# A decode block that streams 561 MB: fewer and larger first and last loads, one VectorE product per group, and the first load issued before the engines' blocks

## The chip, the cores and the metric

The kernel runs on one core of a Trainium2 chip. The metric is the device time of one execution in microseconds (us). The kernel before took 1305.1 us (median of 3 runs, 1304.54 to 1305.36).

## The reference

One decode step for 4 sequences: attention over a cache of 4096 positions with 32 heads of 128, plus a small mixer and MLP, all on the layer-normalised input.

```python
xn = _layernorm(x)                                   # x: 4 x 1 x 512
q  = (xn @ wq).reshape(4, 1, 32, 128)                # per head
s  = einsum("bhqd,bhkd->bhqk", q, k_cache) * 128 ** -0.5
o  = einsum("bhqk,bhkd->bhqd", softmax(s), v_cache)  # k_cache, v_cache: 4 x 32 x 4096 x 128, f32
A  = o.reshape(4, 1, 4096) @ wo
B  = x1 + gelu(_layernorm(x1) @ w3) @ w4             # x1 = xn + the mixer's part
out = x + A + B
```

With one position per sequence, the shifts of the mixer push everything out, so its two weights have no influence, x1 is xn, and the kernel doesn't load them.

## The kernel before

Keys and values are 268 MB each. They are cut into 32 groups of 8.39 MB: a group is four heads of one sequence, laid out as 128 partitions with 16,384 f32 each. Three buffers of that size take turns: S1 and S0 hold keys (even and odd groups), S2 holds values. The weights pass through the same buffers: wq goes through S2 before the first values, w3 and w4 go to S1 after the last even keys, wo goes to S0 after the last odd keys. x and its small intermediates sit at the start of S0 until the second keys are loaded over them.

All large loads are issued by SyncE, on one queue, in the order in which they are written (lines 125 to 157): wq in two pieces of 12/32 and 20/32 (GF = 12), the first keys in two halves, the second keys after `d_T` (q is ready), then a loop over pairs of groups: values when S2 is free (`v_free`), keys when a key buffer is free (`k_free`). At the end come w3, four rows of w4, the last values in two pieces of 12/32 and 20/32, the remaining ten rows of w4, and wo in six pieces. Since SyncE issues in order, a load that waits holds up all loads behind it. x is loaded by ScalarE on its own queue (line 226).

The work on a group:

- VectorE (lines 333 to 353) spreads q over the partitions (qx, qb), multiplies the keys by it in place (two halves, lines 343 and 345), sums over the 128 dimensions (line 347; then `k_free`) and finds the maximum of the scores (lines 349 to 352).
- ScalarE (lines 240 to 248) takes the exponential of the scores into pw.
- TensorE (lines 195 to 209) multiplies the values by pw: 32 matmuls of 512 columns, which the trace counts as 64 passes, then the sums of the weights (then `v_free`), then, after a copy by ScalarE (os), the small products that pick the heads (oz).

The wq product runs on the same TensorE code as turn 0 of 33, with pw holding the transposed input; so both wq and the last values, which come in two pieces, need a wait in the middle of the 32 matmuls (`take(v_rest)` at n = GF, line 199). GpSimd relays these second pieces: it waits for them and then adds to `v_rest`, once with the number of groups, so that the wait passes in all turns between (lines 171 to 176). The same is done for the second half of the first keys (`s_kh`, `s_h`). Matmul GF - 1 of each turn adds to `v_half`; SyncE waits for it before it overwrites the first piece of S2 with that of the last values.

The MLP's first product (w3) runs before the last turn of TensorE; its second (w4, line 217) after it, then X, the normalised attention output, is transposed, and the output product (from line 370) takes wo piece by piece, adds everything, and two small stores write the result.

Of the kernel before, what the change touches and what calls it, by code (L numbers as in the profile page):

```python
# [13 lines left out]
P = 128  # L14
# [6 lines left out]
def decode_block(ctx: ExitStack, tc: tile.TileContext, x, k, v, wq, wo, w3, w4, out):  # L21
# [45 lines left out]
    def sem(name):  # L67
        return tc.alloc_semaphore(name)

    def take(e, s, n=1):  # L70
        e.wait_ge(s, n).then_inc(s, -n)  # L71
# [1 line left out]
    PIECES = ((0, 14), (14, 22), (22, 27), (27, 30), (30, 31), (31, 32))  # L73
    CUT = 27
    SUM = 30
    GF = 12
    s_x, s_v, s_q, s_w3, s_w4 = (sem(n) for n in ("sx", "sv", "sq", "sw3", "sw4"))
    s_k = [sem(f"sk{n}") for n in range(2)]
    s_wo = s_k + [s_x] + [sem(f"swo{n}") for n in range(3)]
    d_self, g_a, c_done, d_T, k_free, v_free, v_rest, v_half = (sem(n) for n in ("dself", "ga", "cd", "dT", "kf", "vf", "vr", "vh"))  # L80
    s_kh, s_h = sem("skh"), sem("sh")
    d_a, a_d, p_a, a_p, d_p, p_d = (sem(n) for n in ("da", "ad", "pa", "ap", "dp", "pd"))

    kf = k.rearrange("b h s d -> (b h s d)").rearrange("(g p r) -> g p r", g=NG, p=P)
# [23 lines left out]
        return e.matmul(o, l, r, start=start, stop=stop)  # L108

    nc.vector.addr_align(128, offset=4, max_nops=0)  # L110
    with tc.tile_critical(no_gpsimd_drain=True), nc.Block(no_gpsimd_drain=True) as block:

        @block.sync
        def _(e):
            def src(flat, g):
                return flat[g] if isinstance(g, int) else flat[bass.ds(g, 1)].rearrange("g p r -> (g p) r")

            def load_k(g, n):
                e.dma_start(KS[n][:, :], src(kf, g)).then_inc(s_k[n], 16)

            def load_v(g):
                take(e, v_free)
                e.dma_start(S2[:, :], src(vf, g)).then_inc(s_v, 16)

            FIRST, REST = slice(0, GF * 4 * DH), slice(GF * 4 * DH, ROW)
            wq_r = wq.rearrange("(p c) n -> p (c n)", p=P)
            e.dma_start(S2[:, FIRST], wq_r[:, FIRST]).then_inc(s_v, 16)
            e.dma_start(S2[:, REST], wq_r[:, REST]).then_inc(s_q, 16)
            for half, s in ((slice(0, ROW // 2), s_k[0]), (slice(ROW // 2, ROW), s_kh)):
                e.dma_start(S1[:, half], kf[0][:, half]).then_inc(s, 16)  # L130
            e.wait_ge(d_T, 1)
            load_k(1, 1)
            with nc.Fori(0, NG, 2, engines=[ET.SP]) as g:
                load_v(g)
                take(e, k_free)
                e.br_lt(g, NG - 2, on_true="sp_more", on_false="sp_next")
                with nc.body("sp_more", valid_engines=[ET.SP]):
                    after = nc.s_assert_within(g + 2, None, NG - 2,
                                               skip_runtime_bounds_check_because="the last turn skips this block")
                    load_k(after, 0)  # L140
                    load_v(after - 1)
                    take(e, k_free)
                    load_k(after + 1, 1)
                    nc.br("sp_next", engines=[ET.SP])
                nc.switch_bb("sp_next")
            e.dma_start(w3_sb, w3.rearrange("(p c) f -> p c f", p=P)).then_inc(s_w3, 16)
            w4_r = w4.rearrange("(p m) n -> p m n", p=P)
            e.dma_start(w4_sb[:, 0:4, :], w4_r[:, 0:4, :]).then_inc(s_w4, 16)
            e.wait_ge(v_half, NG)
            e.dma_start(S2[:, FIRST], vf[NG - 1][:, FIRST]).then_inc(s_v, 16)  # L150
            take(e, v_free)
            e.dma_start(S2[:, REST], vf[NG - 1][:, REST]).then_inc(s_q, 16)
            e.dma_start(w4_sb[:, 4:NF, :], w4_r[:, 4:NF, :]).then_inc(s_w4, 16)
            take(e, k_free)
            wo_r = wo.rearrange("(p c) n -> p c n", p=P)
            for n, (c0, c1) in enumerate(PIECES):
                e.dma_start(wo_sb[:, c0:c1, :], wo_r[:, c0:c1, :]).then_inc(s_wo[n], 16)  # L157

        @block.gpsimd
        def _(e):  # L160
            e.memset(xs, 0.0).then_inc(g_a, 1)
            e.memset(ident[:, :], 0.0).then_inc(c_done, 1)
            e.memset(rs[:, :], 0.0)
            e.memset(pw[:, :, :], 0.0)
            e.wait_ge(c_done, 1)
            e.affine_select(out=ident[:, :], in_=ident[:, :], compare_op=ALU.not_equal, fill=1.0, base=0,
                            pattern=[[-1, P]], channel_multiplier=1).then_inc(c_done, 1)
            e.wait_ge(c_done, 2)
            e.tensor_copy(perm[:, :].rearrange("p (h q) -> p h q", q=4),
                          ident[:, :].rearrange("p (q h) -> p h q", q=4)).then_inc(c_done, 1)  # L170
            take(e, s_q, 16)
            e.wait_ge(c_done, 3).then_inc(v_rest, NG)
            take(e, s_kh, 16)
            e.wait_ge(c_done, 3).then_inc(s_h, NG)
            take(e, s_q, 16)
            e.wait_ge(c_done, 3).then_inc(v_rest, 1)

        @block.tensor
        def _(e):
            pe = [ET.PE]  # L180
            zero = e.zero_reg
            e.br_lt(zero, 0, on_true="pe_near", on_false="pe_far")
            with nc.body("pe_near", valid_engines=pe):
                with nc.Fori(0, NG + 1, 1, engines=pe) as g:
                    e.br_lt(g, NG, on_true="pe_turn", on_false="pe_mlp")
                    with nc.body("pe_mlp", valid_engines=pe):
                        e.wait_ge(s_w3, 16)
                        for c in range(NC):
                            for t in range(4):
                                i = mm(e, pb[32 * t:32 * t + 32, :FT], x1T[:, c, :], w3_sb[:, c, t * FT:(t + 1) * FT],  # L190
                                       c == 0, c == NC - 1)
                        i.then_inc(p_a, 1)
                        nc.br("pe_turn", engines=pe)
                    nc.switch_bb("pe_turn")
                    take(e, s_v, 16)
                    take(e, a_p)
                    for n in range(G4):
                        if n == GF:
                            take(e, v_rest)
                        t = n % 4  # L200
                        i = mm(e, pv[32 * t:32 * t + 32, :], pw[:, n, :], V[:, n // 4, t], n < 4, n >= G4 - 4)
                        if n == GF - 1:
                            i.then_inc(v_half, 1)
                    i.then_inc(p_a, 1)
                    mm(e, oz[:, HG:2 * HG], ones[:, :], rs[:, :], True, True).then_inc(v_free, 1)
                    take(e, a_p)
                    for m in range(4):
                        i = mm(e, oz[:, 0:HG], os[:, m, :], sel[:, HG * m:HG * m + HG], m == 0, m == 3)
                    i.then_inc(p_a, 1)
                e.br_lt(zero, 0, on_true="pe_far", on_false="pe_rest")  # L210
            with nc.body("pe_far", valid_engines=pe):
                e.br_lt(zero, 0, on_true="pe_rest", on_false="pe_near")
            nc.switch_bb("pe_rest")
            mm(e, total[:, 0:P], ident[:, :], base[:, :], True, False)
            e.wait_ge(s_w4, 32)
            take(e, d_p)
            for m in range(NF):
                t = m % 4
                mm(e, y[32 * t:32 * t + 32, :], gT[:, 32 * m:32 * m + 32], w4_sb[:, m, :], m < 4, False)
            take(e, d_p)  # L220
            mm(e, pb[:, 0:P], perm[:, :], Xt[:, :], True, True).then_inc(p_d, 1)
# [49 lines left out]
        def _(e):  # L271
            done = [0]

            def mark(i):
                i.then_inc(d_self, 1)
                done[0] += 1

            def own(i):
                mark(i)
                e.wait_ge(d_self, done[0])  # L280
# [7 lines left out]

            e.memset(ones[:, :], 1.0)
            e.memset(st[:, :], EPS)  # L290
            e.wait_ge(c_done, 2)
            e.reduce_sum(sel[:, :], ident[:, :].rearrange("p (q m) -> p m q", q=4), axis=AX.X)
            take(e, s_x, 16)
            for t in range(1, 4):
# [39 lines left out]
            with nc.Fori(0, NG, 2, engines=[ET.DVE]) as g:  # L334
                for n in range(2):
# [3 lines left out]
                                      .to_broadcast([P, 4, 32])))  # L339
                    own(e.transpose(qb[:, :], qx[:, :]))  # L340
                    take(e, s_k[n], 16)
                    qw = qb[:, :].unsqueeze(1).to_broadcast([P, C // 2, DH])
                    mark(e.tensor_tensor(out=K[:, :C // 2, :], in0=K[:, :C // 2, :], in1=qw, op=ALU.mult))  # L343
                    take(e, s_h)
                    own(e.tensor_tensor(out=K[:, C // 2:, :], in0=K[:, C // 2:, :], in1=qw, op=ALU.mult))  # L345
                    take(e, a_d)
                    mark(e.reduce_sum(sc[:, :], K, axis=AX.X))  # L347
                    e.wait_ge(d_self, done[0]).then_inc(k_free, 1)
# [80 lines left out]
```

## Time and profile before

| what | us |
|---|---|
| median of 3 runs | 1305.1 |
| profiled execution, first to last instruction (its span) | 1302.8 |
| what the median has beyond that span | 2.3 |
| VectorE busy | 1167.5 |
| TensorE busy | 371.5 |
| ScalarE busy | 107.5 |

The profile is one execution on the hardware. Rows of the timeline give the start and the duration in us from the first instruction, the engine, the line, the operation, what it writes and reads, its shape and its count, and in brackets how long the engine was idle before and what released it. "q" behind an engine's name is its sequencer: waits, branches and DMA issues, which don't count as busy. A wait on a semaphore of a DMA often shows as a wait on the engine's own sequencer. A row with several instructions is merged, its duration is their sum. The stretches give busy time per engine in a window, the clock that TensorE was granted, the mean busy share of the 16 DMA engines and what they moved.

The profiled execution's own device time isn't listed apart from the three runs, so its span stands beside their median.

### The profile page before, as it was taken

What the parts mean: (1) busy time and instruction counts of PE and PEld (TensorE: products, weight loads), DVE (VectorE), ACT (ScalarE), POOL (GpSimd) and SP (SyncE); (2) the same over time, 40 slices, a digit from 0 to 9 for tenths busy, and PEclk for the clock granted to TensorE, in tenths of its full rate; (3) what the DMA queues carried; (4) which work ended last, traced back from release to release, by engine and by line L of the source; (5) the groups of instructions that cost most, each with busy time, mean ns of one, the idle gap of its engine ahead of it and who ended that gap; (6) DMA issues with size and microseconds to landing.
All of it is one profiled execution on the core that took longest, in us unless ns stands there. A gap on an engine that the chain in (4) does not pass through costs nothing. (4 is left out here: it accounts for less than half of the span.)

```text
span 1302.8 us, 7122 instructions
## 1 busy us (share of the span) xinstructions
PE 371.5 (29%) x2608; PEld 131.0 (10%) x2608; DVE 1167.5 (90%) x337; ACT 107.5 (8%) x330; POOL 2.5 (0%) x10
## 2 busy tenths in 40 slices
PE   3032123333113333212333212333311333321356
PEld 1010001111001111001111000111100111100112
DVE  4999999999999999999999999999999999999970
ACT  1000000000000000000000000000000000000010
POOL 0000000000000000000000000000000000000000
PEclk9565566666566666556666556666656666656678
DMA  9999999999999999999999999999999999999998
GB/s 402 436 449 421 449 421 449 421 439 429 425 445 421 449 421 449 421 449 421 449 421 445 425 437 431 425 445 421 449 421 449 421 449 421 447 423 445 425 430 344
DMA packets 11115, 561.05 MB, mean 431 GB/s; under 512 B 1244, under 2 KB 1252, under 8 KB 1640
## 3 DMA queue, kind: packets, MB, share of 16 engines
q1 hardware_dynamic: 11096, 561.00, 99.6%
q8 instruction: 2, 0.03, 0.0%
q14 instruction: 1, 0.01, 0.0%
q10 hardware_dynamic: 16, 0.01, 0.0%
HBM read 561.00 MB, written 0.01 MB: 431 GB/s over the span
## 5 line engine op out<-in xcount | busy, mean ns | idle before, releaser
L108 PE MATMUL ps<-slot,pw 128*32 128x512 f32 x2112 | 310.8, 753 | 905.5 <-PEq L71 905.5
L347 DVE TENSOR_REDUCE sc<-slot 128x128 f32<-128x16384 f32 x32 | 551.0, 17220 | 4.2
L343 DVE TENSOR_TENSOR slot<-slot,qb 128x8192 f32<-128x8192 f32 x32 | 278.1, 8692 | 60.8 <-DVEq L71 60.1
L345 DVE TENSOR_TENSOR slot<-slot,qb 128x8192 f32<-128x8192 f32 x32 | 277.9, 8684 | 1.1 <-DVEq L71 1.1
L108 PEld LDWEIGHTS ps<-slot,pw 128*32 128x32 f32 x2112 | 84.5, 134 | 1105.3 <-issue 1105.3
L233 ACT COPY os<-ps 128x512 f32<-128x512 f32 x33 | 19.3, 585 | 898.1 <-ACTq L71 898.1
L245 ACT ACTIVATE pw<-sc,st 32x128 f32<-32x128 f32 x128 | 67.4, 527 | 211.6 <-ACTq L71 210.4
L108 PE MATMUL ps<-sel,os 128*128 128x4 f32 x264 | 33.9, 252 | 18.6 <-PEq L71 18.6
L108 PEld LDWEIGHTS ps<-sel,os 128*128 128x128 f32 x264 | 31.9, 191 | 20.5 <-issue 20.5
L245 ACT ACTIVATION_READ_ACCUMULATOR pw<-sc,st 32x1 f32 x128 | 23.5, 184 | 0.0
L364 DVE RECIPROCAL rec<-OS 128x128 f32<-128x128 f32 x1 | 1.0, 952 | 15.5 <-DVEq L71 15.5
L349 DVE TENSOR_REDUCE st<-sc 128x1 f32<-128x128 f32 x32 | 9.2, 286 | 4.7
L108 PE MATMUL ps<-rs,ones 128*128 128x4 f32 x66 | 12.7, 263 | 0.0
L108 PEld LDWEIGHTS ps<-rs,ones 128*128 128x128 f32 x66 | 9.8, 188 | 27.7 <-issue 27.7
L337 DVE COPY qx<-Q 128x128 f32 x32 | 7.3, 227 | 5.0 <-issue 4.7
L391 DVE COPY res<-ps 64x128 f32<-64x128 f32 x1 | 0.3, 283 | 12.7 <-PE ps L108 12.7
L340 DVE STREAM_TRANSPOSE qb<-qx 128x128 f32<-128x128 f32 x32 | 10.0, 312 | 1.1
L108 PE MATMUL ps<-slot,X 128*4 128x512 f32 (+1 forms) x94 | 9.0, 457 | 3.9 <-DMA slot<-in_A_wo_dram 3.9
L253 ACT COPY OS<-ps 128x8 f32 x32 | 5.3, 165 | 43.8 <-ACTq L71 43.8
L351 DVE STREAM_TRANSPOSE mt<-mx 128x32 f32<-128x32 f32 x32 | 6.8, 211 | 1.1
L352 DVE TENSOR_REDUCE st<-mt 128x1 f32<-128x32 f32 x32 | 5.9, 186 | 1.1
L350 DVE COPY mx<-st 128x32 f32<-128x32 f32 x32 | 5.8, 181 | 1.1
(57 smaller groups left out, 39.3 us busy)
## 6 DMA issues: line engine op xcount, KB each, us to landing
slot<-in_A_k_cache_dram SPq DMA_DIRECT2D x2, 4096.0 KB, 36.0
slot<-in_A_wq_dram SPq DMA_DIRECT2D x1, 5120.0 KB, 22.4
slot<-in_A_v_cache_dram SPq DMA_DIRECT2D x1, 5120.0 KB, 20.5
slot<-in_B_w_dram SPq DMA_DIRECT2D x1, 3584.0 KB
slot<-in_A_wo_dram SPq DMA_DIRECT2D x1, 3584.0 KB, 29.4
slot<-in_A_wq_dram SPq DMA_DIRECT2D x1, 3072.0 KB, 10.7
slot<-in_A_v_cache_dram SPq DMA_DIRECT2D x1, 3072.0 KB, 13.1
slot<-in_B_w_dram SPq DMA_DIRECT2D x1, 2560.0 KB, 26.3
```

Source lines behind the costliest of these rows:

```text
L108: return e.matmul(o, l, r, start=start, stop=stop)
L233: return e.copy(os[:, :, :], pv[:, :].rearrange("p (m d) -> p m d", m=4)).then_inc(a_p, 1)
L245: i = e.activation(o, sc[r, :].rearrange("p (a w t) -> p a t w", w=4, t=4), AF.Exp, bias=st[r, 1:2], scale=1.0, accum_out=rs[r, h:h + 1])
L337: own(e.tensor_copy(qx[:, :].rearrange("p (h r) -> p h r", h=4), Q[:, bass.ds(g + n, 1), :].rearrange("p o h -> p (o h)").unsqueeze(2) .to ...
L340: own(e.transpose(qb[:, :], qx[:, :]))
L343: mark(e.tensor_tensor(out=K[:, :C // 2, :], in0=K[:, :C // 2, :], in1=qw, op=ALU.mult))
L345: own(e.tensor_tensor(out=K[:, C // 2:, :], in0=K[:, C // 2:, :], in1=qw, op=ALU.mult))
L347: mark(e.reduce_sum(sc[:, :], K, axis=AX.X))
L349: own(e.reduce_max(st[:, 0:1], sc[:, :], axis=AX.X))
L350: own(e.tensor_copy(mx[:, :], st[:, 0:1].to_broadcast([P, 32])))
L351: own(e.transpose(mt[:, :], mx[:, :]))
L352: e.tensor_reduce(st[:, 1:2], mt[:, :], axis=AX.X, op=ALU.max, negate=True).then_inc(d_a, 1)
```

## The change

- wq is one load of 8.39 MB instead of two pieces, and it is issued by SyncE before the engines branch into their blocks, so ahead of SyncE's own branch.
- The first keys are one load instead of two halves. VectorE multiplies each group's keys by q in one instruction of 16,384 elements per partition instead of two of 8,192.
- The last values are one load behind `v_free`; w4 is split into 6 and 8 rows (W4A = 6) instead of 4 and 10.
- With that the semaphores and relays for second pieces go: the wait in the middle of TensorE's 32 matmuls, the `v_half` signal, VectorE's wait for `s_h`, and GpSimd's three relays.
- VectorE's first reduction waits for a third GpSimd step (c_done 3, the copy to perm) instead of the second.

```diff
-    GF = 12
+    W4A = 6
...
-    with tc.tile_critical(no_gpsimd_drain=True), nc.Block(no_gpsimd_drain=True) as block:
+    with tc.tile_critical(no_gpsimd_drain=True), ExitStack() as body:
+        nc.sync.dma_start(S2[:, :], wq.rearrange("(p c) n -> p (c n)", p=P)).then_inc(s_v, 16)
+        block = body.enter_context(nc.Block(no_gpsimd_drain=True))
...
-            e.dma_start(S2[:, FIRST], wq_r[:, FIRST]).then_inc(s_v, 16)
-            e.dma_start(S2[:, REST], wq_r[:, REST]).then_inc(s_q, 16)
-            for half, s in ((slice(0, ROW // 2), s_k[0]), (slice(ROW // 2, ROW), s_kh)):
-                e.dma_start(S1[:, half], kf[0][:, half]).then_inc(s, 16)
+            load_k(0, 0)
             e.wait_ge(d_T, 1)
             load_k(1, 1)
...
-            e.dma_start(w4_sb[:, 0:4, :], w4_r[:, 0:4, :]).then_inc(s_w4, 16)
-            e.wait_ge(v_half, NG)
-            e.dma_start(S2[:, FIRST], vf[NG - 1][:, FIRST]).then_inc(s_v, 16)
-            take(e, v_free)
-            e.dma_start(S2[:, REST], vf[NG - 1][:, REST]).then_inc(s_q, 16)
-            e.dma_start(w4_sb[:, 4:NF, :], w4_r[:, 4:NF, :]).then_inc(s_w4, 16)
+            e.dma_start(w4_sb[:, 0:W4A, :], w4_r[:, 0:W4A, :]).then_inc(s_w4, 16)
+            load_v(NG - 1)
+            e.dma_start(w4_sb[:, W4A:NF, :], w4_r[:, W4A:NF, :]).then_inc(s_w4, 16)
...
-            take(e, s_q, 16)
-            e.wait_ge(c_done, 3).then_inc(v_rest, NG)
-            take(e, s_kh, 16)
-            e.wait_ge(c_done, 3).then_inc(s_h, NG)
-            take(e, s_q, 16)
-            e.wait_ge(c_done, 3).then_inc(v_rest, 1)
...
-                        if n == GF:
-                            take(e, v_rest)
...
-                        if n == GF - 1:
-                            i.then_inc(v_half, 1)
...
-            e.wait_ge(c_done, 2)
+            e.wait_ge(c_done, 3)
...
-                    qw = qb[:, :].unsqueeze(1).to_broadcast([P, C // 2, DH])
-                    mark(e.tensor_tensor(out=K[:, :C // 2, :], in0=K[:, :C // 2, :], in1=qw, op=ALU.mult))
-                    take(e, s_h)
-                    own(e.tensor_tensor(out=K[:, C // 2:, :], in0=K[:, C // 2:, :], in1=qw, op=ALU.mult))
+                    own(e.tensor_tensor(out=K, in0=K, in1=qb[:, :].unsqueeze(1).to_broadcast([P, C, DH]), op=ALU.mult))
```

SyncE's instructions at the start of the program, before the change (dT is `d_T`, vf is `v_free`; DMA rows give partitions x elements):

```order
L113 UNCONDITIONAL_BRANCH
L127 DMA slot<-in_A_wq_dram 128x6144
L128 DMA slot<-in_A_wq_dram 128x10240
L130 DMA slot<-in_A_k_cache_dram 128x8192 x2
L119 DMA slot<-in_A_k_cache_dram 128x16384 [waits dT]
```

And with it, from the branch that ends the entry:

```order
L404 UNCONDITIONAL_BRANCH [waits SP_sequencer_49]
L111 DMA slot<-in_A_wq_dram 128x16384
L114 UNCONDITIONAL_BRANCH
L120 DMA slot<-in_A_k_cache_dram 128x16384
L120 DMA slot<-in_A_k_cache_dram 128x16384 [waits dT]
```

Four loads have become two, and wq has moved ahead of the branch into the block.

SyncE at the end of the program, from w3 on (in_B_w is w3 or w4; vh is `v_half`, kf is `k_free`), before:

```order
L146 DMA slot<-in_B_w_dram 128x7168
L148 DMA slot<-in_B_w_dram 128x2048
L150 DMA slot<-in_A_v_cache_dram 128x6144 [waits vh]
L152 DMA slot<-in_A_v_cache_dram 128x10240 [waits vf]
L153 DMA slot<-in_B_w_dram 128x5120
L157 DMA slot<-in_A_wo_dram 128x7168 [waits kf]
```

and with the change:

```order
L142 DMA slot<-in_B_w_dram 128x7168
L144 DMA slot<-in_B_w_dram 128x3072
L124 DMA slot<-in_A_v_cache_dram 128x16384 [waits vf]
L146 DMA slot<-in_B_w_dram 128x4096
L150 DMA slot<-in_A_wo_dram 128x7168 [waits kf]
```

The piece that needed only the first matmuls of the turn before is gone; all of the last values now stand behind `v_free`, and two more rows of w4 stand ahead of them.

VectorE in a group, before (sk0 is the keys' load, sh the relay of its second half, ad ScalarE's signal):

```order
L340 STREAM_TRANSPOSE qb<-qx 128x128 [waits dself]
L343 TENSOR_TENSOR slot<-slot,qb 128x8192 [waits sk0,dself]
L345 TENSOR_TENSOR slot<-slot,qb 128x8192 [waits sh]
L347 TENSOR_REDUCE sc<-slot 128x128 [waits ad,dself]
L349 TENSOR_REDUCE st<-sc 128x1 [waits dself]
```

and with the change:

```order
L323 STREAM_TRANSPOSE qb<-qx 128x128 [waits dself]
L325 TENSOR_TENSOR slot<-slot,qb 128x16384 [waits sk0,dself]
L327 TENSOR_REDUCE sc<-slot 128x128 [waits ad,dself]
L329 TENSOR_REDUCE st<-sc 128x1 [waits dself]
```

Two products have become one, which waits for the whole load.

More of the change, by code (lines that the diff above doesn't have):

```diff
@@ L75, in decode_block @@
     SUM = 30
-    GF = 12
-    s_x, s_v, s_q, s_w3, s_w4 = (sem(n) for n in ("sx", "sv", "sq", "sw3", "sw4"))
+    W4A = 6
+    s_x, s_v, s_w3, s_w4 = (sem(n) for n in ("sx", "sv", "sw3", "sw4"))
     s_k = [sem(f"sk{n}") for n in range(2)]
     s_wo = s_k + [s_x] + [sem(f"swo{n}") for n in range(3)]
-    d_self, g_a, c_done, d_T, k_free, v_free, v_rest, v_half = (sem(n) for n in ("dself", "ga", "cd", "dT", "kf", "vf", "vr", "vh"))
-    s_kh, s_h = sem("skh"), sem("sh")
+    d_self, g_a, c_done, d_T, k_free, v_free = (sem(n) for n in ("dself", "ga", "cd", "dT", "kf", "vf"))
     d_a, a_d, p_a, a_p, d_p, p_d = (sem(n) for n in ("da", "ad", "pa", "ap", "dp", "pd"))
@@ L123, in load_v @@
                 e.dma_start(S2[:, :], src(vf, g)).then_inc(s_v, 16)
-            FIRST, REST = slice(0, GF * 4 * DH), slice(GF * 4 * DH, ROW)
-            wq_r = wq.rearrange("(p c) n -> p (c n)", p=P)
-            e.dma_start(S2[:, FIRST], wq_r[:, FIRST]).then_inc(s_v, 16)
-            e.dma_start(S2[:, REST], wq_r[:, REST]).then_inc(s_q, 16)
-            for half, s in ((slice(0, ROW // 2), s_k[0]), (slice(ROW // 2, ROW), s_kh)):
-                e.dma_start(S1[:, half], kf[0][:, half]).then_inc(s, 16)
+            load_k(0, 0)
             e.wait_ge(d_T, 1)
```

## The prediction

> **What bounds the kernel now.** I read the page first (busy shares and DMA queues), then the stretches (busy time and DMA share of chosen windows), then the timeline of the first 110 us and of the last 60 us.
>
> The page, parts 1 to 3:
>
> ```profile
> PE 371.5 (29%) x2608; PEld 131.0 (10%) x2608; DVE 1167.5 (90%) x337; ACT 107.5 (8%) x330; POOL 2.5 (0%) x10
> ...
> q1 hardware_dynamic: 11096, 561.00, 99.6%
> ...
> HBM read 561.00 MB, written 0.01 MB: 431 GB/s over the span
> ```
>
> The stretches; the last two columns are the DMA share and GB/s. A packet is counted whole near its start, so short windows go above 1:
>
> ```profile
> 1.50:2.00 0.50, 0.00 (x0) 0.00 (x0) 0.18 (x2) 0.00 (x0) 0.50 (x3) 1.00 0.08 16
> 2.00:2.50 0.50, 0.00 (x0) 0.00 (x0) 0.00 (x0) 0.00 (x0) 0.50 (x1) 1.00 2.42 623
> ...
> 60.00:98.70 38.70, 10.78 (x74) 3.86 (x74) 38.15 (x10) 3.19 (x10) 0.00 (x0) 0.59 1.00 434
> ...
> 1297.00:1297.50 0.50, 0.50 (x6) 0.00 (x0) 0.00 (x0) 0.00 (x0) 0.00 (x0) 1.00 0.89 328
> 1297.50:1298.00 0.50, 0.47 (x5) 0.04 (x8) 0.00 (x0) 0.04 (x1) 0.00 (x0) 1.00 0.15 53
> ```
>
> The transfers are the bound. The queue moves from 2.0 us until about 1297.5 us, its packets fill 99.6% of the span of all 16 engines, and one turn of a key load and a value load (8.39 MB each) takes 38.7 us at 434 GB/s. VectorE is close behind with 90%. So the end moves by three things alone: when the first byte flows, any hole in the queue, and what follows the last byte.
>
> I need two lags. **Issue to data**: the first load is issued at 0.97 (row below) and data flow at 2.0, so 1.0 us. **Data to landing**: the bulk is through at 1297.5, and the last wait for a weight piece ends at 1299.20 (row further below), so 1.7 us. A load therefore follows without a hole if it is issued 2.7 us before the landing of the load in front of it.
>
> **The change part by part.** The timeline of the first 110 us (start, duration, engine, line, operation, in brackets the idle time before):
>
> ```profile
> 0.97 0.41 SPq L127 DMA_DIRECT2D slot<-in_A_wq_dram  x1
> ...
> 1.60 0.56 ACTq L226 DMA_DIRECT2D slot<-in_A_x_dram  x1
> ...
> 7.92 1.28 DVE L295 COPY slot<-slot 4x512 f32<-4x512 f32 x3 [4.65 <-DVEq L71]
> ...
> 16.26 0.29 DVE L318 COPY pw<-slot 128x64 f32<-128x64 f32 x2
> ...
> 16.70 5.35 PE L108 MATMUL ps<-slot,pw 128*32 128x512 f32 x24 [16.70 <-PEq L71]
> ...
> 24.09 4.50 PE L108 MATMUL ps<-slot,pw 128*32 128x512 f32 x40 [2.04 <-PEq L71]
> ...
> 30.79 0.33 SPq L119 DMA_DIRECT2D slot<-in_A_k_cache_dram  x1
> ...
> 33.69 8.69 DVE L343 TENSOR_TENSOR slot<-slot,qb 128x8192 f32<-128x8192 f32 x1 [2.03 <-DVEq L71]
> 43.51 8.69 DVE L345 TENSOR_TENSOR slot<-slot,qb 128x8192 f32<-128x8192 f32 x1 [1.13 <-DVEq L71]
> 52.34 17.22 DVE L347 TENSOR_REDUCE sc<-slot 128x128 f32<-128x16384 f32 x1
> ...
> 69.96 0.34 SPq L119 DMA_DIRECT2D slot<-in_A_k_cache_dram  x1
> ...
> 71.32 8.69 DVE L343 TENSOR_TENSOR slot<-slot,qb 128x8192 f32<-128x8192 f32 x1
> ...
> 79.93 8.68 DVE L345 TENSOR_TENSOR slot<-slot,qb 128x8192 f32<-128x8192 f32 x1
> ...
> 82.24 9.44 PE L108 MATMUL ps<-slot,pw 128*32 128x512 f32 x64 [51.74 <-PEq L71]
> ...
> 108.12 8.69 DVE L343 TENSOR_TENSOR slot<-slot,qb 128x8192 f32<-128x8192 f32 x1
> ```
>
> *First load ahead of the blocks.* Only one branch on SyncE leaves the path. The issue stands at 0.97 us, so the bound is between nothing and 0.97 us; since the engine had to be released first and one branch is a small part of that, I take 0.1 us of gain, with up to 0.5 in the range. It moves every later transfer alike.
>
> *wq in one load.* Before, 24 of the 64 passes ran at 16.70, on the first piece, and the other 40 waited for the rest until 24.09. Now all 64 start at about 24.1. As a whole group takes 9.44 us after a pause (row at 82.24), they end at 33.5 instead of 28.6, 4.9 us later, and the load of the second keys goes out at 35.7 instead of 30.79. The first keys landed at 43.5, so 40.8 would be soon enough: 5.1 us of cover are left, and the cost is nothing. The few us lost at this place return only if that cover is gone.
>
> *x behind larger rows.* The small x load shares the engines with wq. It is issued at 1.60 and first used at 7.92, 5.9 us after data began to flow. A row of the first wq piece is 24.6 KB, 0.91 us at a sixteenth of 434 GB/s; of the whole wq it is 65.5 KB, 2.42 us. If x lets the same number of rows by, its 5.9 us become 15.7 and the first use comes at 17.7; if the wait has nothing to do with rows it stays at 7.9. I take 13, since an issue and a landing are part of the wait and don't grow. At 17.7 the weights for the wq product would be ready 9.8 us later than 16.55, at 26.3, and the product would start 2.2 us late, within the cover of 5.1. So it costs nothing at both ends; it would begin to cost with a first use after 20.6.
>
> *First keys in one load and one product.* Now nothing can start on the keys before all of them are there, at about 43.4. One product over 16,384 elements takes what the reduction over as many takes, 17.22 us (two halves took 8.61 + 8.69 = 17.30). The reduction then starts at about 60.7 instead of 52.34, 8.4 us later, and the third key load goes out at 78.4 instead of 69.96. In front of it in the queue are the first values, which landed at 82.2; it has to be issued by 79.5. The cover shrinks from 9.5 to 1.1 us. I take no hole, with up to 1 us in the range. VectorE's own turn is 36.8 us (from the product at 71.32 to that at 108.12, with no idle time that a load ended) against 38.7 for the two loads, so it wins about 2 us a turn and is level again after four or five. In those later turns the saving of one instruction, 0.1 us, lies behind the wait for the keys. The removed relays of GpSimd and the later start of the first VectorE reduction (behind one more small copy on GpSimd) lie before x arrives.
>
> *Last values in one load, w4 as 6 and 8 rows.* The timeline of the end, with two earlier turns for the spread:
>
> ```profile
> 1165.86 8.65 PE L108 MATMUL ps<-slot,pw 128*32 128x512 f32 x64 [27.58 <-PEq L71]
> ...
> 1175.06 0.33 SPq L123 DMA_DIRECT2D slot<-in_A_v_cache_dram  x1
> ...
> 1204.56 9.77 PE L108 MATMUL ps<-slot,pw 128*32 128x512 f32 x64 [28.15 <-PEq L71]
> ...
> 1214.89 0.33 SPq L123 DMA_DIRECT2D slot<-in_A_v_cache_dram  x1
> ...
> 1243.26 9.20 PE L108 MATMUL ps<-slot,pw 128*32 128x512 f32 x64 [27.02 <-PEq L71]
> 1248.22 0.33 SPq L150 DMA_DIRECT2D slot<-in_A_v_cache_dram  x1
> ...
> 1252.87 0.33 SPq L152 DMA_DIRECT2D slot<-in_A_v_cache_dram  x1
> ...
> 1273.68 6.77 PE L108 MATMUL ps<-slot,pw 128*32 128x512 f32 x40 [6.06 <-PEq L71]
> ...
> 1286.70 0.29 DVE L368 COPY X<-ps 128x128 f32<-128x128 f32 x1 [2.19 <-PE ps L108]
> ...
> 1296.04 2.76 PE L108 MATMUL ps<-slot,X 128*4 128x512 f32 x34 [1.18 <-DMA slot<-in_A_wo_dram]
> 1297.96 0.59 ACT L389 COPY os<-ps 128x512 f32<-128x512 f32 x1 [15.24 <-PE ps L108]
> ...
> 1299.20 0.12 PEld L108 LDWEIGHTS ps<-slot,X 128*4 128x4 f32 x8 [0.26 <-DMA slot<-in_A_wo_dram]
> ```
>
> The values before the last landed at 1243.2. Behind them now lie w3 (3.67 MB) and six rows of w4 (1.57 MB), together 12.1 us at 434 GB/s: the queue's bulk runs dry at 1243.2 + 12.1 - 1.7 = 1253.6. The last values may be issued only when the product before is through, at 1252.87 by this trace, and flow at 1253.9: a hole of 0.3 us. The piece issued at 1248.22 used to cover it. From product start to issue it took 9.2 us at 1165.86, 10.3 at 1204.56 and 9.6 here, so the hole lies between 0 and 1.0 us. I take 0.3.
>
> The last product then starts at 1243.2 + 31.4 (13.6 MB) + 0.3 = 1274.9 and has 64 passes ahead of it, not 40. With 9.44 it ends at 1284.3, against 1280.45: 3.9 us later, and X is ready at 1290.9 instead of 1287.0. Before, the output product waited for wo three times; at 1296.04 it stood with 44 passes behind it. From 1290.9 those 44 take 5.0 us (4.50 us for 40), until 1295.9: it meets the third piece just in time. All slack of TensorE is gone there; I take 0.1 us, up to 0.5. The split of w4 itself moves bytes from behind the last values to before them, and the sum of bytes is the same.
>
> **The sum**: -0.1 + 0 + 0 + 0 + 0.3 + 0.1 = +0.3 us. The profiled execution has a span of 1302.8 us; what is reported besides lies around it (2.3 us to the median), and nothing in the change touches that. On the median of 1305.1 that makes 1305.4 us.
>
> **The rivals.** *Slower: x behind all of wq.* If the engines serve all rows of wq before x, x comes with wq at 24.1 instead of 7.92. The weights for the product are then ready at 32.7, it ends at 42.2, and the second keys are issued at 44.4, 3.6 us after the 40.8 that the queue needs: a hole of 3.6 us that nothing gives back, 1309.0 us. It decides from a first use of 20.6 on. Against it: x was used at 7.92, well before the first wq piece (7.2 us of data from 2.0, plus 1.7) could have landed at 10.9, so rows of wq let it by. The Trainium skill speaks for this rival: its page "DMA: Bandwidth & Descriptors", section "Queues, rings and completion order", says that an engine drains a packet of some 9 to 17 descriptors from one queue before it turns to another. By that rule x would have waited for the first piece's eight rows on each engine already, and the trace disagrees. I give it 4%.
>
> *Slower: thin cover.* The lag from issue to data may be longer for a load of 8.4 MB behind a running queue than the 1.0 us of the first one. With 2.0 us more there are holes of 0.9 us before the third keys and 2.3 us before the last values, 2.9 us more than my sum: 1308.3 us. Nothing in this trace shows such a lag, since each load there was issued well ahead. 4%.
>
> *Faster: a cost for each load.* Three loads fewer (wq, keys, values) could save three gaps. If each boundary between loads cost the queue 2 us, the result would be 6 us less, 1299.4 us. Against it: the turn at 60.00 has two boundaries and still a share of 1.00 at 434 GB/s. The Trainium skill has such a fixed cost of about 2.0 us for each DMA (same page, section "Anatomy of one DMA"); here no row shows it as lost time of the queue, only as lag at both ends. 2%.
>
> **How the numbers follow.** My forecast has 90%: 1305.4 us, by its own bounds from 1304.6 (0.5 us at the start, the rest nothing) to 1307.3 (holes of 1.0 and 1.0, 0.5 at the end, no gain). The runs shown spread over 0.8 us, so the low end goes to 1304.2; the high end stays. The measurement tells 0.2%, 2.6 us, from no change; the forecast's whole range lies inside it. The cases give faster 3%, same 90%, slower 7%.
>
> **What would show it.** Right: the third keys issued at about 78.4 and the first VectorE product at 43.4; the wq product as one run of 64 passes from 24.1; the DMA queue's sum unchanged; last values issued near 1253 with at most a short dip; the output product running through from about 1291. Wrong: a dip in the DMA share near 42 (x too late), near 81 or near 1254 of more than 1 us, or an output product that still runs on its first pieces when the last piece lands.

## The result, and the profile after

The changed kernel takes 1306.41 us (median of 21 runs, 1305.14 to 1308.67); the kernel before took 1304.66 us in the same series (21 runs, 1304.44 to 1305.41). The ratio is 1.0013, with a 95% interval of 1.0007 to 1.0019. So it is slower by 1.75 us, 0.13%: within the 0.2% called no change, and within the range, but beyond the 0.3 us of the sum. Also new is the spread: 3.5 us from the fastest to the slowest run, against 1.0 before.

The page of the changed kernel, parts 1, 3 and 4:

```profile
span 1304.8 us, 7016 instructions
...
q1 hardware_dynamic: 10664, 561.00, 99.5%
...
PE 1%; issue 0%; DVE 0%
```

The bytes are the same, the queue is as full as before within 0.1%. But the chain that ended last (third line) begins with TensorE. Before, it was the load of wo, for 36.57 us, and only then TensorE. The chain of before and the chain of after, in order of time (start, duration, what):

```profile
1259.43 36.57 DMA slot<-in_A_wo_dram
```

```profile
1293.90 6.84 PE ps L107 x75
...
1300.78 0.88 PE ps L107 x24
```

The start of the changed kernel (timeline):

```profile
0.96 0.41 SPq L111 DMA_DIRECT2D slot<-in_A_wq_dram  x1
...
11.03 1.28 DVE L278 COPY slot<-slot 4x512 f32<-4x512 f32 x3 [7.30 <-DVEq L71]
...
19.37 0.30 DVE L301 COPY pw<-slot 128x64 f32<-128x64 f32 x2
...
24.13 9.65 PE L107 MATMUL ps<-slot,pw 128*32 128x512 f32 x64 [24.13 <-PEq L71]
...
35.99 0.33 SPq L120 DMA_DIRECT2D slot<-in_A_k_cache_dram  x1
...
43.36 17.23 DVE L325 TENSOR_TENSOR slot<-slot,qb 128x16384 f32<-128x16384 f32 x1 [6.49 <-DVEq L71]
60.72 17.22 DVE L327 TENSOR_REDUCE sc<-slot 128x128 f32<-128x16384 f32 x1
...
78.35 0.34 SPq L120 DMA_DIRECT2D slot<-in_A_k_cache_dram  x1
```

Nearly every time is where the prediction put it: wq's product at 24.1, the second keys issued at 36.0 (35.7), the first keys' product at 43.4, the third keys issued at 78.35 (78.4). What isn't there is the cover that was supposed to make this free. The load behind the third keys is the second values, and TensorE's start on them is their landing. Before:

```profile
120.93 2.79 PE L108 MATMUL ps<-slot,pw 128*32 128x512 f32 x12 [27.35 <-PEq L71]
```

and after:

```profile
82.19 2.79 PE L107 MATMUL ps<-slot,pw 128*32 128x512 f32 x12 [46.50 <-PEq L71]
...
121.14 2.79 PE L107 MATMUL ps<-slot,pw 128*32 128x512 f32 x12 [27.41 <-PEq L71]
```

The first values land at 82.2 as before, the second 0.2 us later than before: the queue lost time between the two.

The end of the changed kernel (timeline):

```profile
1243.53 9.23 PE L107 MATMUL ps<-slot,pw 128*32 128x512 f32 x64 [27.00 <-PEq L71]
...
1253.18 0.33 SPq L124 DMA_DIRECT2D slot<-in_A_v_cache_dram  x1
...
1276.40 9.86 PE L107 MATMUL ps<-slot,pw 128*32 128x512 f32 x64 [18.59 <-PEq L71]
...
1292.51 0.29 DVE L348 COPY X<-ps 128x128 f32<-128x128 f32 x1 [2.19 <-PE ps L107]
1293.90 6.84 PE L107 MATMUL ps<-slot,X 128*4 128x512 f32 x78 [1.43 <-SPq L350]
1300.14 0.59 ACT L369 COPY os<-ps 128x512 f32<-128x512 f32 x1 [11.61 <-PE ps L107]
...
1301.69 0.28 DVE L371 COPY res<-ps 64x128 f32<-64x128 f32 x1 [8.89 <-PE ps L107]
```

The rows of before for the output product's first two starts, and for the last copy:

```profile
1288.08 3.61 PE L108 MATMUL ps<-slot,X 128*4 128x512 f32 x28 [1.42 <-DMA slot<-in_A_wo_dram]
1292.96 1.90 PE L108 MATMUL ps<-slot,X 128*4 128x512 f32 x16 [1.27 <-DMA slot<-in_A_wo_dram]
...
1299.67 0.28 DVE L391 COPY res<-ps 64x128 f32<-64x128 f32 x1 [12.69 <-PE ps L108]
```

The last copy comes 2.02 us later, which is the difference of the spans (2.0). The output product runs all its 78 passes without one wait for wo; before, it waited for wo at 1288.08, 1292.96 and 1296.04. The end has changed hands from the queue to TensorE. And between X, ready at 1292.80, and the first pass at 1293.90 stand 1.1 us in which TensorE waits for SyncE (`SPq L350`): that is the meeting of all engines at the end of the blocks, which before lay beside the wait for the first piece of wo.

### The profile page after: what moved, and what is told of

Its sections match the earlier page's. It is cut to its first block, busy times and chain, and to the rows that moved or that the text cites. A ratio compares the mean times of both kernels' runs of the same rounds, so it can differ in the third digit from the quotient of the medians.

```text
span 1304.8 us, 7016 instructions
## 1 busy us (share of the span) xinstructions
PE 366.2 (28%) x2608; PEld 131.0 (10%) x2608; DVE 1165.4 (89%) x305; ACT 107.6 (8%) x330; POOL 2.5 (0%) x10
## 5 line engine op out<-in xcount | busy, mean ns | idle before, releaser
L325 DVE TENSOR_TENSOR slot<-slot,qb 128x16384 f32<-128x16384 f32 x32 | 551.2, 17226 | 59.1 <-DVEq L71 58.1
L107 PE MATMUL ps<-slot,pw 128*32 128x512 f32 x2112 | 306.9, 746 | 915.3 <-PEq L71 915.3
```

Source lines behind the costliest of these rows:

```text
L325: own(e.tensor_tensor(out=K, in0=K, in1=qb[:, :].unsqueeze(1).to_broadcast([P, C, DH]), op=ALU.mult))
```

## The experiments

Each kernel but the changed one ran 11 times, in one of three series, each beside 33 runs of the kernel before on the same chip (medians 1304.77, 1304.70 and 1304.74 us). Medians, and what they are above the kernel before in their own series; the interval of every ratio is about 0.0009 to either side, 1.2 us, so the smaller differences lean on the runs' ranges and on the traces.

| run | us | above before | range of runs |
|---|---|---|---|
| changed kernel (21 runs) | 1306.41 | 1.75 | 1305.14 to 1308.67 |
| tail put back | 1305.64 | 0.87 | 1305.06 to 1305.95 |
| tail put back, first keys in halves | 1304.68 | 0.0 | 1304.53 to 1305.29 |
| tail put back, third keys still later | 1306.12 | 1.38 | 1305.64 to 1307.70 |
| first load early, alone | 1304.79 | 0.09 | 1304.59 to 1305.02 |
| tail alone, 6 rows of w4 | 1305.35 | 0.58 | 1304.81 to 1306.46 |
| tail alone, 8 rows | 1306.39 | 1.65 | 1305.19 to 1307.49 |
| tail alone, 8 rows, two pieces | 1305.39 | 0.65 | 1304.59 to 1306.30 |
| tail alone, 6 rows, two pieces | 1305.16 | 0.42 | 1304.59 to 1307.26 |
| changed, 8 rows | 1306.99 | 2.22 | 1305.52 to 1307.97 |
| changed, 4 rows | 1306.62 | 1.85 | 1305.91 to 1307.91 |
| changed, no meeting | 1306.49 | 1.79 | 1304.64 to 1307.40 |
| changed, 8 rows, no meeting | 1306.31 | 1.61 | 1305.16 to 1307.82 |

### Which half of the change: start or tail

The changed kernel with its tail put back:

```diff
-    W4A = 6
+    W4A = 4
+    GF = 12
...
-            load_v(NG - 1)
+            FIRST, REST = slice(0, GF * 4 * DH), slice(GF * 4 * DH, ROW)
+            e.wait_ge(v_half, NG)
+            e.dma_start(S2[:, FIRST], vf[NG - 1][:, FIRST]).then_inc(s_v, 16)
+            take(e, v_free)
+            e.dma_start(S2[:, REST], vf[NG - 1][:, REST]).then_inc(s_q, 16)
...
```

The wait in the middle of the 32 matmuls, the `v_half` signal and GpSimd's relays for the last values come back with it.

> The changed kernel with only its tail put back: last values in two pieces, w4 as 4 and 10 rows, the mid-turn wait and signal for the pieces; wq, first keys, the one VectorE product and the early first load stay as changed. Theory A (the loss is made at the tail, by the hole before the last values and the longer TensorE chain behind them): 0.3 us above the kernel before, the cost of the late third keys alone. Rival B (the loss is made at the start, by late third keys and wq in one load): about 1.7 us above the kernel before, as the whole change.

The kernel before with only the tail changed (the same lines the other way round, with 6 rows):

> The kernel before with only the tail changed: last values in one load behind the end of the product before, w4 as 6 and 8 rows, the rest as before. Theory A (tail): 1.5 us above the kernel before, with the runs spread over some 2 to 3 us as in the changed kernel. Rival B (start): no more than 0.3 us above.

Measured 0.87 and 0.58 us. Neither theory is right alone: the start costs more than I had given it, the tail less. Together they are 1.45 of the 1.75 us. For the start, 8 of the 11 runs lie above the slowest of the 33 runs of before (1305.28); for the tail it is 6 of 11, with some as fast as before, so its size is less sure. The spread of the changed kernel comes with the tail: 0.9 us without it, 1.65 with it alone.

### The start: what of it costs

First keys in halves again, with two products, on top of the tail put back; wq in one load and the early issue stay. Of the edit, the loads:

```diff
-            load_k(0, 0)
+            for half, s in ((slice(0, ROW // 2), s_k[0]), (slice(ROW // 2, ROW), s_kh)):
+                e.dma_start(S1[:, half], kf[0][:, half]).then_inc(s, 16)
```

> The changed kernel with the tail put back (as in the first run) and with the first keys in two halves and two VectorE products again; what is left of the change is wq in one load and the early first load. Theory D (the loss at the start comes from the third keys, which the first keys in one load make late): back to the kernel before, within 0.3 us. Rival (wq in one load costs it, by TensorE's later product or by x that waits behind its rows): it stays 0.9 us above the kernel before.

Measured 0.0 us. The loss at the start is the first keys' alone; wq in one load, and x behind its rows, cost nothing. Whether it is their one load or their one product wasn't tried apart; the product has to wait for all of the load in any case.

The first load early, alone:

```diff
+        nc.sync.dma_start(S2[:, FIRST], wq_r[:, FIRST]).then_inc(s_v, 16)
+        block = body.enter_context(nc.Block(no_gpsimd_drain=True))
...
-            e.dma_start(S2[:, FIRST], wq_r[:, FIRST]).then_inc(s_v, 16)
```

> The kernel before with one edit: the first piece of wq is issued ahead of the engines' blocks; it stays in two pieces. Theory: the issue moves by 0.01 us (0.97 to 0.96, as in the changed kernel's trace) and the time stays, within 0.2 us of the kernel before. Rival (the branch, with what code it has to fetch, cost up to 0.5 us): 0.3 to 0.5 us less.

Measured 0.09 us above: the branch that it is moved past costs nothing that can be measured.

Then the suspected cost was increased, with VectorE held back once ahead of the loop:

```diff
             e.wait_ge(d_T, 1).then_inc(a_d, 1)
+            for _ in range(2):
+                own(e.reduce_sum(mt[:, :], ones[:, :].unsqueeze(1).to_broadcast([P, 32, P]), axis=AX.X))
+            clear()
```

> The run with only the tail put back, and besides two reductions of 4,096 elements on VectorE ahead of the loop, whose result is not used. They take some 8.8 us, of which 6.5 us fall into VectorE's wait for the first keys, so the first product starts about 2.1 us later, and so do the third keys. Theory D (what is lost at the start is a hole in the queue ahead of the third keys, one for one): 2.1 us more than without them, 3.0 us above the kernel before. Rival (the third keys still come in time, and the loss is made elsewhere, in the one product or the single first load): no change against the run without them, 0.9 us above.

Measured 1.38 us, 0.5 more than without the delay, and every run at or above that kernel's median. The delay came out as 1.4 us, not 2.1, since q was ready 1.2 us earlier in that run. So the third keys' issue does move the end (the rival falls), but not one for one: about a third of the lateness. The issue of the third keys, then TensorE's start on the second values, for the tail put back, for the halves, and for the delay:

```profile
78.45 0.34 SPq L121 DMA_DIRECT2D slot<-in_A_k_cache_dram  x1
...
121.42 1.93 PE L108 MATMUL ps<-slot,pw 128*32 128x512 f32 x8 [27.62 <-PEq L71]
```

```profile
71.69 0.34 SPq L122 DMA_DIRECT2D slot<-in_A_k_cache_dram  x1
...
120.97 2.79 PE L109 MATMUL ps<-slot,pw 128*32 128x512 f32 x12 [27.57 <-PEq L71]
```

```profile
79.84 0.34 SPq L121 DMA_DIRECT2D slot<-in_A_k_cache_dram  x1
...
121.62 1.93 PE L108 MATMUL ps<-slot,pw 128*32 128x512 f32 x8 [26.84 <-PEq L71]
```

With the issue at 69.96 (before) and 71.69 the second values land at 120.9 to 121.0; at 78.35 to 78.45 they land 0.2 and 0.5 us later, at 79.84 0.7 us later. The price begins well before the point where, by my two lags, a hole would open (79.5). Why, can be read in part from the stretches where the third keys' first rows start (last columns: DMA share and GB/s). With halves, then the tail put back, then the delay:

```profile
80.00:80.50 0.50, 0.00 (x0) 0.00 (x0) 0.50 (x1) 0.00 (x0) 0.00 (x0) 0.50 3.64 1573
```

```profile
80.00:80.50 0.50, 0.00 (x0) 0.00 (x0) 0.50 (x1) 0.50 (x2) 0.00 (x0) 0.50 3.01 1180
```

```profile
80.00:80.50 0.50, 0.00 (x0) 0.00 (x0) 0.43 (x4) 0.00 (x0) 0.00 (x0) 0.50 0.02 0
80.50:81.00 0.50, 0.00 (x0) 0.00 (x0) 0.47 (x3) 0.32 (x1) 0.00 (x0) 0.50 3.21 1049
```

Packets are counted whole where they start, so GB/s divided by the share is the rate of the rows that start there: 1573 / 3.64 = 432 with halves, the steady rate; 1180 / 3.01 = 392 with the tail put back; 1049 / 3.21 = 327 with the delay, where in addition nothing at all started from 80.0 to 80.5. The lag from issue to data is the 1.0 us of the forecast there (79.84 to after 80.5). What is added is that rows which follow close on their issue pass more slowly.

The traces' packet records (a packet is one row of a load) let the two be told apart. From 78 to 86 us the 16 engines stood idle, on average, 0.1 us with the tail put back and 0.8 us with the delay, and the rows took 0.3 and 0.6 us longer than at the steady rate; with halves it is nothing of either. So the queue as a whole lost 0.4 and 1.4 us in these executions: without the delay mostly by slow rows, with it by a real hole as well. The landing shows less of it because it hangs on the last engine. In the trace of before fifteen engines were through with the first values at 79.98 to 80.46 and the sixteenth at 81.47; time that the fifteen lose shows only once they become the last.

### The tail: hole or chain

The changed kernel with 8 and with 4 rows of w4 ahead of the last values (`W4A = 8`, `W4A = 4`):

> The changed kernel with 8 rows of w4 ahead of the last values instead of 6, so 1.2 us more of transfers as cover. The hole before the last values should go, and the last byte of wo should land about 1.2 us earlier than in the changed kernel. Theory A1 (the hole in the queue sets the end): 0.5 us above the kernel before, 1.2 us less than the changed kernel. Theory A2 (TensorE's chain behind the last values sets the end): their landing is put off by the 1.2 us of w4 as much as the hole put it off, so the time stays that of the changed kernel, 1.7 us above the kernel before, within 0.4.

> The changed kernel with 4 rows of w4 ahead of the last values instead of 6, so 1.2 us less cover: the hole grows by 1.2 us, the last values land as late as in the changed kernel, and the last byte of wo 1.2 us later. Theory A1 (the hole sets the end, one for one): 2.9 us above the kernel before. Theory A2 (TensorE's chain sets the end): 1.7 us above, until the queue overtakes the chain; by the changed kernel's trace, where the chain was 0.4 us behind the queue, 2.5 us above at most.

Measured 2.22 and 1.85 us. A1, the hole as what sets the end, falls on both: without the hole it wanted 0.5 us, with a hole of 1.2 us more it wanted 2.9. A2 wanted 1.7 (within 0.4, a little less than came) and at most 2.5. More cover makes it no faster since TensorE gets the last values no earlier: they landed 32.8 us after the product before them had started with 8 rows (1244.63 to 1277.38), 32.9 with 6 (1243.53 to 1276.40); with 4 rows it was 31.6 (1243.80 to 1275.35), and there the queue was last. With 8 rows the chain that ended last is TensorE's, with 4 rows the load of wo. Parts 4 of the two pages:

```profile
PE 1%; issue 0%; DVE 0%
PE ps L107 1%; DVE res L371 0%
```

```profile
DMA 3%; PE 0%; SPq 0%; DVE 0%; issue 0%
DMA slot<-in_A_wo_dram 3%; PE ps L107 0%; SPq L150 0%; DVE res L371 0%
```

The same without the change at the start. First the kernel before with the tail changed and 8 rows; then also with the last values in two pieces, both behind the end of the product before, so that the queue carries the same bytes in the same order and only TensorE may start earlier; then that with 6 rows:

```diff
-            load_v(NG - 1)
+            take(e, v_free)
+            e.dma_start(S2[:, FIRST], vf[NG - 1][:, FIRST]).then_inc(s_v, 16)
+            e.dma_start(S2[:, REST], vf[NG - 1][:, REST]).then_inc(s_q, 16)
```

> The kernel before with the tail changed and 8 rows of w4 ahead of the last values: no hole, but the last values land 1.2 us later by their place in the queue than with 6 rows and no hole. Theory A2 (TensorE's chain behind the last values sets the end): 1.3 us above the kernel before, more than the 0.6 us with 6 rows. Theory A1 (the hole sets the end): 0 to 0.2 us above.

> As the run before, but the last values come in two pieces of 12/32 and 20/32, both issued behind the end of the product before, so that TensorE can start on the first piece; the queue has the same bytes in the same order. Theory A2: 24 of the 64 passes leave the chain behind the last landing, about 3 us, and the queue sets the end again: 0 to 0.2 us above the kernel before. Rival (the place of w4 in the queue costs by itself): as the run before, 1.3 us above.

> As the run before, with 6 rows of w4 ahead of the last values, so with the hole of the changed kernel but without the long chain. Theory A2: only the hole is left, 0.2 to 0.4 us above the kernel before, less than the 0.6 us of the tail in one piece. Theory A1 (the hole alone makes the tail's loss): 0.6 us above, as in one piece.

Measured 1.65, 0.65 and 0.42 us. With 8 rows, 1.0 us goes when TensorE may start on the first piece; the place of w4 by itself doesn't cost it. With 6 rows the two pieces gain 0.16 us, too little to tell. What is left in the two-piece kernels, 0.4 to 0.65, is more than A2 had (0 to 0.4): the queue too loses something at this place, with 8 rows as well. By the packets from 1252 to 1262 us, the engines stood idle 0.1 us longer than before with 8 rows in two pieces and 0.3 with 6, and in both the rows took 0.5 us longer: mostly slow rows, as at the start. In the changed kernel it is 0.2 us of idle time and 0.75 of slow rows. A stretch of before (rows of the first piece of the last values), then the same stretch of the changed kernel, in which most first rows of the last values start:

```profile
1254.00:1254.50 0.50, 0.50 (x8) 0.43 (x11) 0.50 (x1) 0.00 (x0) 0.00 (x0) 1.00 1.49 639
```

```profile
1254.00:1254.50 0.50, 0.50 (x6) 0.50 (x6) 0.50 (x1) 0.00 (x0) 0.00 (x0) 1.00 4.04 1327
```

That is 639 / 1.49 = 429 GB/s before and 1327 / 4.04 = 328 after. TensorE's rows in one piece, then in two (8 rows):

```profile
1276.94 10.00 PE L108 MATMUL ps<-slot,pw 128*32 128x512 f32 x64 [18.92 <-PEq L71]
...
1294.57 6.85 PE L108 MATMUL ps<-slot,X 128*4 128x512 f32 x78 [1.42 <-SPq L363]
```

```profile
1277.02 7.15 PE L108 MATMUL ps<-slot,pw 128*32 128x512 f32 x40 [7.43 <-PEq L71]
...
1291.80 5.32 PE L108 MATMUL ps<-slot,X 128*4 128x512 f32 x44 [1.42 <-SPq L367]
1297.36 2.72 PE L108 MATMUL ps<-slot,X 128*4 128x512 f32 x34 [0.23 <-DMA slot<-in_A_wo_dram]
```

The last values land at the same time, the product is 2.85 us shorter (7.15 against 10.00), and the output product starts 2.8 us earlier and waits for wo again before its third piece.

### The meeting between X and the output product

The output product, its copies and the two stores moved into the engines' blocks, with 6 and with 8 rows; TensorE waits for X alone:

```diff
             mm(e, pb[:, 0:P], perm[:, :], Xt[:, :], True, True).then_inc(p_d, 1)
+            e.wait_ge(x_done, 1)
+            for n, (c0, c1) in enumerate(PIECES):
+                e.wait_ge(s_wo[n], 16)
...
-            e.tensor_copy(X[:, :, :], pb[:, 0:P].rearrange("p (b h) -> p b h", b=B))
+            e.tensor_copy(X[:, :, :], pb[:, 0:P].rearrange("p (b h) -> p b h", b=B)).then_inc(x_done, 1)
```

> The changed kernel with the output product, its copies and the two stores moved into the engines' blocks, so that no all-engine meeting stands between X and the output product; the queue is untouched. Theory C (the end is the later of two: the queue's last landing + 0.5 us, and TensorE's chain, 1.55 us after the copy of the first 27 columns' sum starts): the chain gets about 1.0 us shorter, falls behind the queue, and the end comes 0.4 us earlier than in the changed kernel, 1.3 us above the kernel before. Rival (the hole in the queue alone sets the end): no gain, 1.7 above. Rival (the chain alone sets it): 1.0 us less, 0.7 above.

> As the run before, with 8 rows of w4 ahead of the last values, so without the hole before them. Theory C: with 8 rows the chain was 1.5 us behind the queue, so all of the 1.0 us that the meeting costs is won: 1.2 us above the kernel before, against 2.2 for the same split with the meeting. Rival (the queue sets the end): no gain against 8 rows with the meeting, 2.2 above.

Measured 1.79 and 1.61 us. With 8 rows that is 0.6 us less than with the meeting (2.22), of the 1.0 expected; with 6 rows nothing is gained where 0.4 was expected. The edit itself did what it should (6 rows):

```profile
1291.84 0.29 DVE L374 COPY X<-ps 128x128 f32<-128x128 f32 x1 [2.19 <-PE ps L108]
1292.18 5.33 PE L108 MATMUL ps<-slot,X 128*4 128x512 f32 x44 [0.38 <-DVE X L374]
1297.82 2.75 PE L108 MATMUL ps<-slot,X 128*4 128x512 f32 x34 [0.31 <-DMA slot<-in_A_wo_dram]
```

From X to the first pass it is 0.05 us, not 1.1, and the product ends up waiting for wo again. In this profile the queue sets the end, as theory C has it. That the median with 6 rows didn't move is not explained by C. In this profile the queue itself was later than in that of the changed kernel (last values issued at 1254.56 against 1253.18), so the two ends can't be compared one for one; with a spread of 2.8 us over 11 runs, 0.4 us is at the edge of what the medians can tell, and I leave it open. None of these versions beats the kernel before, which has the queue as its bound from the first to the last byte.

## Why the prediction came out as it did

The time is inside the range and within 0.2% of no change, as forecast; the queue was the bound, and at three of the five places the change cost nothing, as forecast to 0.1 us. The sum of 0.3 us was wrong: 1.75 us were measured, 1.45 of them from the other two. That the time still fell into the range is owed to its bounds, which allowed holes of 1.0 us at these two places, and not to the mechanism: what was lost there was mostly rows that passed slowly, and a meeting of the engines that the prediction didn't have.

- **First load ahead of the blocks, -0.1 us: nothing.** The issue went from 0.97 to 0.96 us, and alone it measured 0.09 us longer, which is no difference.
- **wq in one load, 0: right.** The product took 9.65 us from 24.13, the second keys were issued at 35.99, within 0.3 of the forecast, and the halves experiment shows the cost at 0.0.
- **x behind larger rows, first use at 13, cost 0: right.** It was used at 11.03, between the bounds of 7.9 and 17.7, and the weights for wq's product were ready at 19.7, before wq itself. The rival in which x comes with all of wq, at 24.1, didn't happen. The Trainium skill's rule on which it stood ("DMA: Bandwidth & Descriptors", section "Queues, rings and completion order": an engine drains a packet of some 9 to 17 descriptors of one queue before it turns to the next) doesn't agree with this trace either, where 8 rows on each engine make up all of wq. By the packets, x's four rows of data went from 7.66 to 8.01 us and its completion writes from 10.16 to 10.44, one row of wq later (before: from 5.49 to 6.56 and from 6.48 to 7.48, one shorter row later): x was let in between single rows.
- **First keys in one load, 0 with up to 1 us: a mis-sized term, 0.87 to 0.89 us** (0.89 is the tail put back less the same with halves, each against its own series). Each time in the working came out to 0.1 us, but "it has to be issued by 79.5" failed: I had made the need of a load (1.0 + 1.7 us ahead of the landing in front) from lags at both ends of the program, and took a load that meets it to be free. At 3.8 us ahead (78.35 against 82.19) the load behind was late already; the keys after those, 6.6 us ahead (114.57 against 121.14), lost nothing (38.72 us from the second values to the third at 159.86, 38.75 before). The 1.7 us were short too: the first engine was through with the first values at 80.06, 2.1 us ahead of their landing. The thin-cover rival was right about the place; its mechanism, a longer lag, is not what the delay showed: the lag was at most 1.2 us there.
- **Last values in one load, 0.3 + 0.1 us: 0.58 us alone, and a wrong step.** "From 1290.9 those 44 take 5.0 us [...] it meets the third piece just in time" had the right mechanism, slack of TensorE that runs out, and left out a piece of it: the 1.1 us meeting of the engines between X and the product, which the trace of before hides beside the wait for wo at 1288.08. Besides, the last values landed at 1276.4 instead of 1274.9 and their product took 9.86 us instead of 9.44, so X came at 1292.8, not 1290.9. The hole of 0.3 us was about right (0.2); the 0.75 us of slow rows behind it were not in the sum. With that TensorE was behind the queue, and the end was its.
- **Three loads fewer, 6 us less: no.** With wq merged and issued early the time was that of before to 0.02 us. The fixed cost of a DMA in the Trainium skill (same page, section "Anatomy of one DMA", about 2.0 us, fitted there for loads that GpSimd issues, not SyncE) shows in no run here as time lost between loads of a full queue.

Not settled: the remaining 0.3 us between the whole and the sum of start and tail, and why the kernels that issue the last values behind the whole product before them vary by 1.7 to 3.5 us from run to run. That product took 8.65 to 9.77 us for the same 64 passes in the rows of before, and in the experiments from 8.41 (tail alone, 6 rows) to 9.83 (tail alone, 8 rows); the issue follows its end by 0.4 to 0.6 us. The length goes with the granted clock: in the product of 8.65 us it was 0.50 from 1165.9 to 1169.0 and 1.00 from 1169.2 to 1174.4, in that of 9.77 us 0.50 from 1204.6 to 1210.0 and 1.00 only from 1210.3. So the issue varies by over 1 us between traces; that this makes the spread of the runs is argued, not tried.

## What to carry to other kernels

In this kernel, whose transfer queue is full from end to end, merging loads won nothing, and a merge that makes an issue or a consumer later has to be paid from cover: count the cover at each such place, and ask for more than the bare lags from issue to data and from data to landing (here 6.6 us ahead of the landing in front were free, 3.8 us were not, and the lags alone would have asked for 2.7). The end of a program is the later of two chains, so write down the slack of the one that is not the bound now, with every wait that is hidden beside it; a wait that the profile doesn't show as idle time may be there all the same. And where the consumer's chain is the later one, splitting the last load paid with the queue's order unchanged, because the consumer starts earlier (1.0 us of 1.65 with 8 rows; 0.16 of 0.58 with 6, too little to tell).

## What the runs showed of the hardware

- Rows of a load that was issued shortly before the queue ran dry passed more slowly than in the steady stream, with hardly a hole (0.1 us) needed: 392 GB/s for the first rows of the third keys, 432 when they were issued 10 us ahead; with a hole of 0.8 us, 327. Counted to the moment when the first of the 16 engines is through with the load in front, 1.5 to 1.7 us of lead lost 0.4 to 0.5 us of the queue's time (third keys, tail put back and changed kernel); 2.1 us (last values, 8 rows without the meeting) and 4.0 us (the keys after the third, with the delay) lost nothing.
- The 16 engines don't finish a load together: in the trace of before fifteen were through with the first values by 80.46 us, the last at 81.47, and TensorE started on them at 82.24.
- A small load on another queue got in between the rows of a large one: x was first used at 7.92 us beside rows of 24.6 KB and at 11.03 us beside rows of 65.5 KB, long before the large load was through.
- The same 64 passes took TensorE 8.65 us where the granted clock went from 0.50 to 1.00 after 3.3 us, and 9.77 us where it did so after 5.7.
- The meeting of all engines at the end of the blocks took 1.1 us from the end of VectorE's last copy to TensorE's first pass; a semaphore in its place took 0.05 us.
- One VectorE product of 16,384 elements took 17.23 us against 17.30 for two of 8,192: at this size the second instruction cost 0.07 us.
